# Sorting v of batch 0 straight from its token-major rows, in a Sinkhorn attention and feed-forward kernel

## The chip, the cores and the metric

The kernel runs on one core of one Trainium2 chip. The metric is device time in microseconds (us): 268.45 us is the median of three runs before the change (267.92 to 269.1).

## The reference

A doubly normalised 8x8 matrix P per batch and head mixes the eight 96-token blocks of k and of v. Each block of q then attends to its own mixed block only, and the result goes through a two-layer feed-forward network.

```python
B, H, S, D = 4, 8, 768, 64;  n_blocks = 8;  block = 96
P = sort_net
for _ in range(5):
    P = P - np.max(P, axis=-1, keepdims=True)
    P = np.exp(P)
    P = P / (np.sum(P, axis=-1, keepdims=True) + 1e-09)
    P = P / (np.sum(P, axis=-2, keepdims=True) + 1e-09)
k_sorted = np.einsum('bhij,bhjcd->bhicd', P, k_b)      # k_b, v_b: [B, H, 8, 96, 64]
v_sorted = np.einsum('bhij,bhjcd->bhicd', P, v_b)
scores = (1 / np.sqrt(D)) * np.matmul(q_b, k_sorted.transpose(0, 1, 2, 4, 3))
attn = softmax(scores)                                  # over the 96 keys of the block
x = np.matmul(attn, v_sorted)                           # to [3072 tokens, 512]
h = x @ w_in                                            # [512, 2048]
out = (np.maximum(h, 0) + alpha * np.minimum(h, 0)) @ w_out   # [2048, 512]
```

## The kernel before

**Layout of v.** Each batch of q, k and v is loaded by one DMA (four for batch 3) from GpSimd's queue, which converts float32 to bf16 on the way. It lands as 128 partitions by 3072 elements. A partition is one half of one block of one head: 48 tokens of 64 elements each. For v this tile is `VST` (two of them, used in turn by even and odd batches); within a partition an element of the head dimension, d, recurs every 64 elements.

**Sorting v.** `conv_v(b, u)` copies eight of the 64 values of d from `VST` into `VD`, a tile of 64 rows of d by 64 tokens: the 48 tokens of each d become contiguous, and the 16 elements behind them stay zero from a clearing at the start (the key `VD0`). `prep_v(b, u)` is a group of 16 matmuls: for each of eight d, and for both halves of the blocks, the stationary operand is the 64 elements of this d in `VD`, the moving operand is every second column of `BDK` (P spread as a block-diagonal 128x128 matrix per batch). The two halves go to partitions 0 to 63 and 64 to 127 of a PSUM bank, so the zero tokens fill the rows between. A copy on ScalarE (ACT) or VectorE (DVE), at line 538 (L538, recorded by the profile under the helper's L323), then evicts the bank into `VS`, from which attention takes it. Eight groups, u = 0 to 7, make a batch. For batch 0 they use four banks in turn (psO0, psO1, psP, psY); later batches use psP alone.

**Batch 0 at the start.** Loads of q, k and v of batch 0 come first. Meanwhile the Sinkhorn loop (`sinkhorn`) runs on DVE and ACT, and TensorE (PE) runs fill-in matmuls on an identity matrix (L811), which write psY and are put in PE's holes up to the first group of `prep_v` that uses psY, and again between the first unit of the first feed-forward layer and the first of the second. `prep_q` and `prep_k` (recorded at L486) write the head-dimension-major QTz and KT. Blocks 0 and 1 then go through `attention`: scores (L569), maximum (L575, tile nm), scores once more less the maximum (L590, L581), exponential (L613, tile Es0), product with `VS` (L622), reciprocal and scaling (L627, L630, tile xq), transposition on PE (L645) into xT.

**Feed-forward.** `ffn1` (L666, with L676 on ACT and L679 on DVE) makes one 128-row unit of the hidden layer for a chunk of blocks: two blocks for the first two chunks, four for the others. `ffn2` (L700) makes 128 output tokens. They fill PE beside attention.

**Order.** Nothing is ordered by hand. Every operation is added to a graph with its engine (or `EITHER`: ACT or DVE), an assumed duration, a priority (lower first) and the keys that it reads and writes. `schedule` then walks through time: on the engine that can start first, it takes the operation of lowest priority number among those ready within 60 ns. It models DMAs from GpSimd's queue as one sequence with assumed durations. The result is a fixed order for each engine; every engine runs its order and waits on semaphores, so an operation that waits holds up all behind it on its engine. On GpSimd (POOL) computing operations and DMA issues share one such order.

Priorities around the change: q -98, k -97 and v -96 of batch 0 are loaded; `VD` is cleared at -95.5; `prep_q` -50, `prep_k` -47, the attention scores of blocks 0 and 1 -46.5 and -46.375, `conv_v` -45.5, `prep_v` -45. Then on POOL: clearing QN and loading k of batch 1 at -21, clearing Esb at -20.5, eight loads of q at -20, v of batch 1 at -19, v of batch 2 at -12, k of batch 2 at -11.9. The weights are loaded at -40 to -29. The load of v of batch 2 overwrites the tile of batch 0 and so waits for whatever reads it.

Of the kernel before, what the change touches and what calls it, by code (L numbers as in the profile page):

```python
# [7 lines left out]
AP = bass.AP  # L8
ACTF = mybir.ActivationFunctionType
BF16 = mybir.dt.bfloat16  # L10
# [231 lines left out]
def bass_sinkhorn_attn__then__act_prelu_kernel(  # L242
# [11 lines left out]
    G = _Graph()  # L254
    sems = {e: es.enter_context(nc.semaphore("s_" + e)) for e in ENGS}

    def dma_sem(name):
        return [es.enter_context(nc.semaphore("d_" + name)), 0]

    def sb(name, shape, dt):  # L260
        return es.enter_context(nc.sbuf_tensor(name, shape, dt))
# [4 lines left out]
    PE, ACT, DVE, POOL, SYNC = ("pe",), ("act",), ("dve",), ("pool",), ("sync",)  # L266
# [14 lines left out]
    BDK = sb("BDK", [128, 4, 128], BF16)  # L281
# [8 lines left out]
    QS = [sb("QS0", [128, 3072], BF16)]  # L290
    QN = sb("QN", [128, 6, 8, 128], BF16)
    KS = [sb("KS%d" % n, [128, 3072], BF16) for n in range(2)]
    VST = [sb("VST%d" % n, [128, 3072], BF16) for n in range(2)]
    VD = sb("VD", [128, 64, 64], BF16)
    QTz = [sb("QTz%d" % n, [128, 2, 4, S], BF16) for n in range(2)]
    KT = [sb("KT%d" % n, [128, 4 * NB * BK0], BF16) for n in range(2)]
# [25 lines left out]
    def copy(e, o, i):  # L322
        return e.activation(o, i, ACTF.Copy) if e is nc.scalar else e.tensor_copy(o, i)  # L323

    def t_either(n, mode=1):
# [4 lines left out]
          w=["P"], prio=-100, dma=(dma_sem("sn"), 0))  # L330
# [12 lines left out]
    def paced(g, n):  # L343
        return [(("turned", "turnx")[n % 2], g + n // 2)]
# [22 lines left out]
    def load_kv(t, src, name, sem, g, b, prio):  # L367
        n = 4 if b == 3 else 1
        for x in range(n):
            G.add(POOL, lambda e, x=x: e.dma_start(  # L370
                AP(t[b % 2], x * 3072 // n, [[3072, 128], [1, 3072 // n]]),
                AP(src.tensor, b * HB + x * 3072 // n, [[3072, 128], [1, 3072 // n]])),
                load_us / n, r=paced(g, x) * (b == 3), w=[(name, b % 2), (name, b % 2, x)] if x == 0 else [(name, b % 2, x)],
                prio=prio, dma=(sem[b + x], 0))

    def load_k(b, prio):
        load_kv(KS, k, "KS", d_k, 11, b, prio)

    def load_v(b, prio):
        load_kv(VST, v, "VST", d_v, 9, b, prio)  # L380

    def consts():
        G.add(DVE, lambda e: e.memset(identf[:, :], 1.0), 150, w=["identf"], prio=-90)
        G.add(POOL, lambda e: e.affine_select(identf[:, :], identf[:, :], [[-1, 128]],
                                              AluOpType.is_equal, 0.0, base=0, channel_multiplier=1),
              350, r=["identf"], w=["identf"], prio=-96.5)
        ib = G.add(ACT, lambda e: copy(e, identb[:, :], identf[:, :]), 280, r=["identf"], w=["identb"],
                   prio=-90)
        G.add(DVE, lambda e: e.memset(epst[:, :], EPS), 100, w=["eps"], prio=-89)
        G.add(POOL, lambda e: e.memset(AP(VD, 48, [[4096, 128], [64, 64], [1, 16]]), 0.0), 900,  # L390
              w=["VD0"], prio=-95.5)
        for h in range(H):
            G.add(POOL, lambda e, h=h: e.memset(  # L393
                AP(QN, h * 128 + (1 - h // 4) * 64, [[6144, 128], [1024, 6], [1, 64]]), 0.0),
                400, w=[("QN0", h)], prio=-21)
        G.add(DVE, lambda e: e.memset(AP(VS[1], 64, [[64 * 65, 112], [65, 64]]), 0.125), 200, w=[("VS1", 1)], prio=-30)

        def red(o, src, w):
            G.add(DVE, lambda e: e.reduce_sum(o, src, axis=AxisListType.X), 280, r=["identf"], w=[w],
                  prio=-70)  # L400
        red(AP(mk1, 0, [[16, 128], [2, 8], [1, 2]]),
            AP(identf, 0, [[128, 128], [16, 8], [1, 2], [2, 8]]), "mk1")
        G.add(ACT, lambda e: e.activation(mkh[:, :], mk1[:, :], ACTF.Copy, scale=0.125), 200, r=["mk1"], w=["mkh"],
              prio=-67)
        for n in range(NE):
            G.add(POOL, lambda e, n=n: e.memset(AP(Esb[n], 48, [[1024, 96], [64, 16], [1, 16]]), 0.0), 300,
                  w=[("Epad", n)], prio=-20.5)
        G.add(DVE, lambda e: e.tensor_reduce(mkj[:, :], AP(identf, 0, [[128, 128], [2, 8], [16, 8], [1, 2]]),
                                             AxisListType.XY, AluOpType.add), 280,
              r=["identf"], w=["mkj"], prio=-70)  # L410
        G.add(DVE, lambda e: e.tensor_reduce(one0[:, :], AP(identf, 0, [[128, 112], [64, 2], [1, 48]]),
                                             AxisListType.XY, AluOpType.add), 280,
              r=["identf"], w=["one0"], prio=-70)
        G.add(ACT, lambda e: e.activation(AP(VS[0], 64, [[64 * 65, 112], [65, 64]]), AP(one0, 0, [[1, 112], [0, 64]]),
                                          ACTF.Copy, scale=0.125),
              220, r=["one0"], w=[("VS1", 0)], prio=-60)
        G.add(ACT, lambda e: copy(e, AP(selk, 0, [[512, 32], [16, 32], [1, 16]]),
                                  AP(identf, 0, [[128, 32], [1, 32], [0, 16]])), 600,
              r=["identf"], w=["selk"], prio=-66)
        return ib.idx  # L420
# [93 lines left out]

    def conv_v(b, u, prio):
        o = AP(VD, 8 * u * 64, [[4096, 128], [64, 8], [1, 48]])
        i = AP(VST[b % 2], 8 * u, [[3072, 128], [1, 8], [64, 48]])
        G.add(EITHER, lambda e: copy(e, o, i), {"act": 845, "dve": 480},
              r=[("VST", b % 2)] + [("VST", b % 2, x) for x in range(4)], w=[("VD", u)], prio=prio)

    def prep_v(b, u, prio, bank=BANK_P):
        t, off, row, keys = bank
        n = b % 2

        def f(e):
            inst = None
            for dd in range(8):
                for th in range(2):
                    inst = e.matmul(AP(t, th * 64 * row + off + dd * 64, [[row, 64], [1, 64]]),  # L529
                                    AP(VD, (8 * u + dd) * 64, [[4096, 128], [1, 64]]),  # L530
                                    AP(BDK, b * 128 + th, [[512, 128], [2, 64]]))
            return inst
        op = G.add(PE, f, 8 * 33, r=[("VD", u), "VD0", ("BDK", b)], w=keys, prio=prio)
        if keys == ["psY"]:
            first_y.append(op)
        o = AP(VS[n], 8 * u, [[64 * 65, 112], [65, 64], [1, 8]])
        i = AP(t, off, [[row, 112], [1, 64], [64, 8]])
        G.add(EITHER, lambda e: copy(e, o, i), {"act": 685, "dve": 690}, r=keys + [("VS1", n)], w=[("VS", n, u)],  # L538
              prio=prio)
# [177 lines left out]
    load_k(0, -97)  # L717
    load_v(0, -96)
    ident_op = consts()
    sinkhorn()  # L720
    spread([0], -48)
# [2 lines left out]
    for u in range(6):  # L724
        prep_k(0, u, -47, BANKS0[(u + 1) % 5])
    for u in range(8):
        conv_v(0, u, -45.5)
    for u in range(8):
        prep_v(0, u, -45, (BANK_O + [BANK_P, BANK_Y])[u % 4])
    for p in range(4):  # L730
        G.add(POOL, lambda e, p=p: e.dma_start(  # L731
# [3 lines left out]
    for p in range(2):  # L735
# [6 lines left out]
          r=["alphaR", "identf"], w=PSP, prio=-44)  # L742
    G.add(DVE, lambda e: e.tensor_scalar(out=omaT[:, :], in0=AP(psYP, 512, [[1024, 128], [1, 16]]), scalar1=-1.0,
                                         scalar2=1.0, op0=AluOpType.mult, op1=AluOpType.add), 200,
          r=PSP, w=["omaT"], prio=-44)
# [4 lines left out]
    for ga, gb in chunks:  # L750
        w = gb - ga
# [11 lines left out]
    for g in range(NG + 12):  # L763
# [9 lines left out]
        b, i = g // NB, g % NB  # L773
# [10 lines left out]
        if b + 1 < B:  # L784
            for t in range(6 if b == 0 and i == 1 else 0):
                turn_q(1, t, 2 + t / 2)
            if b > 0 and i < 6:
                turn_q(b + 1, i, 8 * b + 2 + i / 2)
            vu = [(conv_v, b + 1, u) for u in range(3)]
            for u in range(8):  # L790
                vu += [(prep_v, b + 1, u)] + [(conv_v, b + 1, u + 3)] * (u < 5)
            units = [(prep_k, b + 1, u) for u in range(6)]
            units = units + vu if b == 0 else vu + units
            for x in range(len(units)):
                if i == (4 + x * 4 // len(units) if b == 0 else 1 + x * 7 // len(units)):
                    f, *a = units[x]
                    f(*a, x * 5 / len(units) if b == 0 else 8 * b + 2 + x * 5 / len(units))
# [56 lines left out]
```

## Time and profile before

| | us |
|---|---|
| median of three runs | 268.45 (267.92 to 269.1) |
| the profiled execution, its own time | 268.33 |
| its span in the profile | 266.6 |
| PE busy | 243.1 (91%) |
| DVE busy | 173.8 (65%) |
| ACT busy | 158.5 (59%) |
| POOL busy | 38.8 (15%) |
| `conv_v`, all batches: 19 on DVE, 13 on ACT | 0.526 and 0.870 each (medians) |
| v of a batch, from issue to landing (median of three) | 29.2 |
| mean granted clock of PE | 0.966 |

The profile records one execution. Times are counted from the span's start; "busy" excludes waiting, branching and issuing DMAs. PE is matmuls, PEld weight loads, which overlap with them; SP is the engine that issues output stores and transposing DMAs. In a line of the timeline, the first number is the start, the second the length from the first to the last of the "xN" instructions merged in it, and "[... <-X]" gives idle time of the engine just before, with what ended it ("issue": nothing that the profile shows). A letter-digit name such as L529 is a line of the kernel. The clock is the share of full speed that PE was granted.

### The profile page before, as it was taken

The numbers are of one execution on the slowest core, as the hardware profiler recorded it, in microseconds if no ns is written. First come the engines' busy times: TensorE is split into PE (matmuls) and PEld (weight loads), VectorE is DVE, ScalarE is ACT, GpSimd is POOL, SyncE is SP. The second block draws the span as 40 slices with busy tenths as digits, with TensorE's granted clock in tenths as the row PEclk, the third lists the DMA queues.
The fourth block names the chain that finished last, engine by engine and source line by source line (L and its number), as shares of the span: only waits on it lengthen the run. The fifth ranks groups of instructions, "written<-read, shape, count | busy, mean of one in ns | idle before, by whom it ended". The sixth has DMA issues, their size and how long they took to land.

```text
span 266.6 us, 6349 instructions
## 1 busy us (share of the span) xinstructions
PE 243.1 (91%) x2634; PEld 148.4 (56%) x2665; DVE 173.8 (65%) x344; ACT 158.5 (59%) x425; POOL 38.8 (15%) x62
## 2 busy tenths in 40 slices
PE   4797899789999987999999999998998899999995
PEld 1376677556755654555565555554654545555542
DVE  5787667957955976687885757874666666445400
ACT  4385445747887885677795366564757765444411
POOL 8994000000900111064000000000000000000000
PEclk9997599959999999999999999999999999999999
DMA  6999999999976999999897412524524272000122
GB/s 100 216 202 195 201 207 175 212 187 176 88 104 122 123 163 148 242 142 171 105 140 158 59 54 71 123 48 113 122 52 95 46 100 70 23 37 36 39 81 80
DMA packets 76926, 32.17 MB, mean 121 GB/s; under 512 B 67792, under 2 KB 72928, under 8 KB 76896
## 3 DMA queue, kind: packets, MB, share of 16 engines
q0 software_dynamic: 25168, 13.63, 41.8%
q1 hardware_dynamic: 51728, 18.11, 35.6%
q8 instruction: 21, 0.34, 0.5%
q14 instruction: 9, 0.07, 0.1%
HBM read 27.28 MB, written 6.29 MB: 126 GB/s over the span
## 4 chain that ended last, share of the span: by engine, by line
PE 66%; DMA 11%; DVE 8%; POOL 7%; ACT 4%; issue 2%; POOLq 0%
PE psH L666 27%; PE psYP L700 25%; DMA VST<-in_v_dram 11%; PE psS L700 4%; PE psO L622 3%; PE psYP L529 3%; DVE hT L679 3%; POOL QN L352 3%; ACT Esb L602 2%; PE psS L566 2%; PE psYP L486 1%; DVE xq L630 1%; POOL QN L393 1%; POOL w_in_bf L731 1%; ACT t L676 1%
## 5 line engine op out<-in xcount | busy, mean ns | idle before, releaser
L679 DVE SCALAR_TENSOR_TENSOR hT<-t,omaT,psH 128x384 bf16<-128x384 f32 (+1 forms) x139 | 77.1, 571 | 42.7 <-ACT t L676 41.5
L666 PE MATMUL psH<-xT,w_in_bf 128*128 128x384 bf16 (+1 forms) x556 | 98.8, 314 | 2.7 <-DVE hT L679 2.1
L676 ACT ACTIVATE t<-psH 128x384 f32<-128x384 f32 (+1 forms) x139 | 62.2, 465 | 48.6 <-PE psH L666 47.5
L700 PE MATMUL psYP<-w_out_bf,hT 128*128 128x512 bf16 x306 | 79.3, 382 | 5.3 <-DVE hT L679 1.2
L666 PEld LDWEIGHTS psH<-xT,w_in_bf 128*128 128x128 bf16 x556 | 50.2, 99 | 37.1 <-DVE hT L679 7.9
L602 ACT ACTIVATE Esb<-psS,nf 96x96 bf16<-96x96 f32 x192 | 46.2, 342 | 8.3 <-DVE nf L575 8.2
L700 PEld LDWEIGHTS psYP<-w_out_bf,hT 128*128 128x128 bf16 x336 | 31.6, 99 | 33.4 <-DVE outstg L323 2.5
L352 POOL DMA_DIRECT2D QN<-in_q_dram x24 | 20.2, 864 | 45.2 <-DMA QTz<-QN 44.3
L575 DVE TENSOR_REDUCE nf<-psS 96x8 f32<-96x768 f32 x24 | 22.7, 948 | 5.9 <-PE psS L566 5.8
L630 DVE TENSOR_TENSOR xq<-psO,rec 96x512 bf16<-96x512 f32 x31 | 21.3, 686 | 0.9
L323 ACT ACTIVATE outstg<-psYP 128x512 f32<-128x512 f32 x16 | 9.6, 599 | 10.0 <-PE psYP L700 10.0
L529 PE MATMUL psYP<-BDK,VD 128*64 128x64 bf16 x448 | 12.9, 204 | 1.4 <-DVE VS L323 0.9
L811 PE MATMUL psYP<-identb 128*128 128x512 bf16 x36 | 11.1, 445 | 3.4 <-ACT identb L323 3.4
L323 ACT ACTIVATE VS<-psYP 112x512 bf16<-112x512 f32 x15 | 10.3, 685 | 5.7 <-PE psYP L529 5.4
L529 PEld LDWEIGHTS psYP<-BDK,VD 128*64 128x64 bf16 x448 | 9.9, 117 | 6.6 <-issue 1.9
L566 PEld LDWEIGHTS psS<-KT,QTz 128*96 128x96 bf16 x192 | 11.5, 124 | 3.6 <-ACT Esb L602 1.2
L566 PE MATMUL psS<-KT,QTz 128*96 128x96 bf16 x192 | 12.8, 210 | 0.5 <-ACT Esb L602 0.5
L622 PEld LDWEIGHTS psO<-VS,ET 112*96 112x96 bf16 x192 | 11.9, 125 | 2.5
L627 DVE RECIPROCAL rec<-psO 96x8 f32<-96x8 f32 x31 | 6.2, 200 | 10.0 <-PE psO L622 9.7
L622 PE MATMUL psO<-VS,ET 112*96 112x65 bf16 x192 | 12.4, 209 | 0.0
L323 DVE CAST VS<-psYP 112x512 bf16<-112x512 f32 x13 | 9.0, 690 | 4.8 <-PE psYP L529 4.8
L323 ACT ACTIVATE VD<-VST 128x384 bf16<-128x384 bf16 x13 | 10.8, 872 | 0.9 <-PE psYP L529 0.5
(108 smaller groups left out, 179.7 us busy)
## 6 DMA issues: line engine op xcount, KB each, us to landing
out_dram<-outstg SPq DMA_DIRECT2D x24, 256.0 KB, 2.1
KS<-in_k_dram POOLq DMA_DIRECT2D x3, 768.0 KB, 28.6
VST<-in_v_dram POOLq DMA_DIRECT2D x3, 768.0 KB, 29.2
QN<-in_q_dram POOLq DMA_DIRECT2D x24, 96.0 KB, 5.0
w_in_bf<-in_moe_w_in_dram POOLq DMA_DIRECT2D x4, 512.0 KB, 17.4
w_out_bf<-in_moe_w_out_dram POOLq DMA_DIRECT2D x2, 1024.0 KB, 27.3
QS<-in_q_dram POOLq DMA_DIRECT2D x1, 768.0 KB, 6.9
VST<-in_v_dram POOLq DMA_DIRECT2D x4, 192.0 KB, 4.7
```

Of the source, the lines that this page charges most:

```text
L323: return e.activation(o, i, ACTF.Copy) if e is nc.scalar else e.tensor_copy(o, i)
L352: G.add(POOL, lambda e, h=h: e.dma_start(AP(QN, h * 128 + (h // 4) * 64, [[6144, 128], [1024, 6], [1, 64]]), AP(q.tensor, b * HB + h * S * ...
L529: inst = e.matmul(AP(t, th * 64 * row + off + dd * 64, [[row, 64], [1, 64]]), AP(VD, (8 * u + dd) * 64, [[4096, 128], [1, 64]]), AP(BDK, b ...
L566: inst = e.matmul(o, AP(QTz[n], hp * 3072 + h4 * 768 + i * 96, [[6144, 128], [1, 96]]), AP(KT[n], (h4 * 8 + i) * bk, [[ld, 128], [64, 2], ...
L575: G.add(DVE, lambda e: e.tensor_reduce(AP(nx, 0, [[8, 96], [4, 2], [1, 4]]), AP(psX, 0, [[1024, 96], [512, 2], [96, 4], [1, 96]]), AxisLis ...
L602: inst = e.activation(AP(Esb[me], p * 128, [[1024, 96], [64, 2], [1, 48]]), AP(psX, (p // 4) * 512 + (p % 4) * 96, [[1024, 96], [48, 2], [ ...
L622: inst = e.matmul(AP(psZ, hp * 512 + h4 * 68, [[1024, 96], [1, 65]]), AP(ET[me] if far else Es0[m], pos(h4, hp) * 96, [[768, nk], [1, 96]] ...
L630: G.add(DVE, lambda e: e.tensor_tensor(out=AP(xq[me], 0, [[512, 96], [256, 2], [64, 4], [1, 64]]), in0=AP(psZ, 0, [[1024, 96], [512, 2], [ ...
L666: inst = e.matmul(AP(pt, poff, [[1024, 128], [1, n]]), AP(w_in_bf, kt * DFF + ft * 128, [[KT_TILES * DFF, 128], [1, 128]]), AP(xT, kt * XR ...
L676: G.add(ACT, lambda e: e.activation(AP(t1[tb], 0, [[384, 128], [1, n]]), AP(pt, poff, [[1024, 128], [1, n]]), ACTF.Relu, scale=-1.0), t_ac ...
L679: G.add(DVE, lambda e: e.scalar_tensor_tensor(out=AP(hT, ft * RING + tok % RING, [[FT_TILES * RING, 128], [1, n]]), in0=AP(t1[tb], 0, [[38 ...
L700: inst = e.matmul(AP(bank[0], bank[1], [[row, 128], [1, 512]]), AP(hT, ft * RING + tok % RING, [[FT_TILES * RING, 128], [1, 128]]), AP(w_o ...
```

## The change

For batch 0 alone, `prep_v` takes its stationary operand from `VST` itself: the 64 elements that start at d and step by 64. The tile `VST0` is widened from 3072 to 4096 elements a partition, and its last 1024, which are tokens 48 to 63, are cleared at the start by POOL, in the place where `VD` was cleared. The clearing of `VD`, which later batches still need, moves to priority -20.7. The eight `conv_v` of batch 0 are gone. Batches 1 to 3 are sorted as before; batch 2 uses the widened tile through `conv_v`.

```diff
@@ -290,7 +290,7 @@
-    VST = [sb("VST%d" % n, [128, 3072], BF16) for n in range(2)]
+    VST = [sb("VST%d" % n, [128, VP], BF16) for n, VP in ((0, 4096), (1, 3072))]
@@ -368,7 +368,7 @@ def load_kv
-                AP(t[b % 2], x * 3072 // n, [[3072, 128], [1, 3072 // n]]),
+                AP(t[b % 2], x * 3072 // n, [[4096 if name == "VST" and b % 2 == 0 else 3072, 128], [1, 3072 // n]]),
@@ -387,8 +387,10 @@ def consts
+        G.add(POOL, lambda e: e.memset(AP(VST[0], 3072, [[4096, 128], [1, 1024]]), 0.0), 900,
+              w=["VST0"], prio=-95.5)
         G.add(POOL, lambda e: e.memset(AP(VD, 48, [[4096, 128], [64, 64], [1, 16]]), 0.0), 900,
-              w=["VD0"], prio=-95.5)
+              w=["VD0"], prio=-20.7)
@@ -514,7 +516,7 @@ def conv_v
-        i = AP(VST[b % 2], 8 * u, [[3072, 128], [1, 8], [64, 48]])
+        i = AP(VST[b % 2], 8 * u, [[3072 if b % 2 else 4096, 128], [1, 8], [64, 48]])
@@ -527,10 +529,11 @@ def prep_v
                     inst = e.matmul(AP(t, th * 64 * row + off + dd * 64, [[row, 64], [1, 64]]),
+                                    AP(VST[0], 8 * u + dd, [[4096, 128], [64, 64]]) if b == 0 else
                                     AP(VD, (8 * u + dd) * 64, [[4096, 128], [1, 64]]),
                                     AP(BDK, b * 128 + th, [[512, 128], [2, 64]]))
             return inst
-        op = G.add(PE, f, 8 * 33, r=[("VD", u), "VD0", ("BDK", b)], w=keys, prio=prio)
+        op = G.add(PE, f, 8 * 33, r=[("VST", 0), "VST0", ("BDK", 0)] if b == 0 else [("VD", u), "VD0", ("BDK", b)], w=keys, prio=prio)
@@ -723,8 +726,6 @@
-    for u in range(8):
-        conv_v(0, u, -45.5)
     for u in range(8):
         prep_v(0, u, -45, (BANK_O + [BANK_P, BANK_Y])[u % 4])
```

## The prediction

> **What bounds the kernel now.** I read the summary lines of the page first, for which engine is full, and where it is not.
>
> ```profile
> span 266.6 us, 6349 instructions
> PE 243.1 (91%) x2634; PEld 148.4 (56%) x2665; DVE 173.8 (65%) x344; ACT 158.5 (59%) x425; POOL 38.8 (15%) x62
> PE   4797899789999987999999999998998899999995
> PEclk9997599959999999999999999999999999999999
> ```
>
> PE is busy for 91% of the span, so time is made where PE has holes or a slow clock. Each digit is a slice of 6.67 us. The holes stand in slices 0 to 5 (to 40 us) and 9 to 10 (60 to 73 us), and the granted clock is down in slices 3 and 4 and again in slice 8. The change works in slices 2 and 3. The timeline of that stretch comes next, one engine at a time.
>
> ```profile
> 16.84 1.12 DVE L323 COPY VD<-VST 128x384 bf16<-128x384 bf16 x2
> 19.63 1.10 DVE L323 COPY VD<-VST 128x384 bf16<-128x384 bf16 x2
> 20.67 1.27 DVE L323 CAST VS<-psO 112x512 bf16<-112x512 f32 x2
> ...
> 17.32 3.19 ACT L323 ACTIVATE VD<-VST 128x384 bf16<-128x384 bf16 x4
> ...
> 17.96 0.72 PE L529 MATMUL psO<-BDK,VD 128*64 128x64 bf16 x32
> 22.89 0.57 PE L529 MATMUL psO<-BDK,VD 128*64 128x64 bf16 x20 [1.12 <-issue]
> 25.11 0.85 PE L622 MATMUL psO<-VS,Es 112*96 112x65 bf16 x8 [0.16 <-DVE VS L323]
> ```
>
> Columns are start, length, engine, line, operation. Conversions hold DVE and ACT from 16.84 to 20.7, the first eviction of sorted v into VS therefore starts at 20.67, the last ends at 25.05, and the first attention product (L622) starts at 25.11, released by it. PE has a hole of 1.12 us inside this, at 21.77, for which the profile shows no releaser. Third, the chain of waits in order of time, and the table by stretches (columns: stretch, length, busy time and count of PE, PEld, DVE, ACT, POOL, clock, DMA share, GB/s):
>
> ```profile
> 21.36 29.17 DMA VST<-in_v_dram
> 50.53 0.02 issue
> 50.55 2.25 DVE VD L323 x5
> ...
> 20.27:23.67 3.40, 2.10 (x67) 1.84 (x67) 2.43 (x5) 2.80 (x5) 2.73 (x5) 0.95 1.24 206
> 23.67:27.08 3.41, 2.52 (x44) 2.15 (x39) 2.35 (x7) 0.89 (x2) 0.00 (x0) 0.50 1.21 181
> 27.08:30.50 3.42, 2.98 (x27) 2.09 (x27) 2.26 (x5) 1.31 (x3) 0.00 (x0) 0.50 1.22 200
> 30.50:33.90 3.40, 3.40 (x27) 2.49 (x27) 1.75 (x6) 1.36 (x3) 0.00 (x0) 0.55 1.24 207
> 51.06:54.47 3.41, 1.27 (x24) 0.74 (x17) 3.38 (x9) 2.94 (x6) 0.00 (x0) 0.94 1.05 212
> ```
>
> The chain does not go through the start: it runs through the load of v of batch 1, landing at 50.53. So a gain at 25 us has to pass that point. And the clock is at half from about 23.7 to 33.7, after a stretch in which PE was busy 2.10 of 3.40 us.
>
> **The change part by part.** *The conversions* (L726-727) go: four DVE copies, 1.12 + 1.10 = 2.22 us, and four ACT copies, 3.19 us.
>
> *The matmuls* (L529) stay 8 groups of 16; each now waits for the load of v alone. That had landed by 16.84, when the first conversion read it. Three groups can be put where three fill-in matmuls stood (16.71 to 17.47), as their banks (two of psO, psY) are free or nearly so, while the first scores still wait for the KT eviction that ends at 17.42. From here I lay the queues out by hand. A group in a run of two adds 0.72 - 0.44 = 0.28 us, a group by itself about 0.33; I take 0.33 for the old operand.
>
> *The price of the operand.* The stationary operand is now read with a step of 64 elements, 128 bytes; no weight load of this trace does that. Lower end 0: a group whose moving operand steps by two elements (L529) and one with a step of one (L486) both take 0.44 us. It can't be below 0, as the count and size of loads stay. Upper end: ACT takes 0.872 us for the 384 elements of a conversion, read with this step, against 0.49 us for an xT copy of 384 read in order; 0.38/384 = 1.0 ns an element, 64 ns a load, 128 loads: 8.2 us. DVE's two rows (0.526 against 0.36) give 0.43 ns, 28 ns a load, 3.5 us. The nearest row is the same group on PE itself with the whole array at half clock: 0.64 us at 59.04 against 0.44 at full clock. If the step halves the rate of the loads, it costs at most that 0.20 a group, 1.6 us in all; since loads of one half of the array run beside matmuls of the other I take half, 0.10 a group, 0.8 us, and a group of 0.43.
>
> *The queues then.* PE: groups 0, 1 and 3 from 16.84 to 18.13, both scores (0.56) to 18.7, group 2 to 19.1, then 4 and 5 as their banks come free. Evictions cost 0.69 each. ACT takes u0 at 17.5, u3 at 18.3, u2 at 19.3 and u4 to 20.7; DVE takes u1 to 18.6, the two maxima (0.95 each) to 20.4, and u5, u6 and u7 to 22.5. The exponentials (0.82, 0.81) of blocks 0 and 1 follow their maxima and end near 21.5 and 22.4, where they were at 21.2 and 22.06. So VS is full at 22.5, not 25.05, and L622 starts at 22.6: 2.5 us earlier. The hole of 1.12 us has no cause that I can take away, so I keep all of it: **1.4 us**. The point at which this is zero: 2.5 us over eight groups, 0.31 us a group or 19 ns a load above 0.43 with the hole gone, 0.18 us a group with it.
>
> *The clock.* It came back after 30.50:33.90, in which PE had no hole, not after 27.08:30.50, with 2.98 of 3.42. L666 now starts 1.4 us earlier, at 27.8 instead of 29.17, and that earlier stretch is then close to full (30.5 - 27.8 = 2.7, and about 0.5 before it). If the clock returns one stretch sooner, PE, which has no hole there, gains half of 3.4 us, 1.7. I take half of that, **0.85 us**, since 3.2 of 3.42 lies between what did and what did not bring it back.
>
> The Trainium skill gives a rule for this: "TensorE: Matmul & The Clock Gate", Part 1, has the clock decided in free-running windows of 3413 ns. The changes here at 23.7, 33.7 to 33.9 and 54.5 agree, with three and nine such windows between them. By the rule the gain is 1.7 or 0, never 0.85, and the sum below would be 3.1 or 1.4.
>
> A second rule speaks against the change: "SBUF — State Buffer", the box on cachelines under Door 1, wants two hits in each 16-byte line for full bandwidth, and this operand has one. It gives no duration; were the loads to run at half rate with nothing hidden, the price is 1.6 us in place of 0.8 and the sum is 0.8 us smaller.
>
> *POOL.* The clearing of VST0's tail takes the place and size of the old clearing of VD (0.97 us at 3.43). VD's own moves behind the QN clearings; queued behind it on POOL are three Esb clearings, eight q loads, then v of batch 1, k and v of batch 2, all 0.97 us later. I cost that at nothing: v of batch 1 was issued at 21.36 and landed 29.17 us later, with 175 to 212 GB/s in every slice between; it waits for its turn. Should the queue run dry, 0.97 us comes back at 50.5. The load of v of batch 2 waits now for PE's last group instead of a conversion; it is issued about when it was (22.43), and first read at 60.28.
>
> *At 50.5.* The conversions of batch 1 wait there, 0.3 us in ACT. The planner (`schedule`) times loads by a sequence of their own, so with an earlier start it places more work ahead of these conversions rather than pulling them ahead of the load, and there is some: 13 of the 32 feed-forward units of blocks 0 to 3 come after 50 us. I take off **0.25 us** for a longer wait.
>
> Sum: 1.4 + 0.85 - 0.25 = 2.0. The profiled execution took 268.33 us (span 266.6 and 1.7 around it), so 266.3; the median of the runs is 0.12 higher, so **266.4 us**. About 0.5% (1.3 us) is what a measurement of this kernel can tell from no change: faster is below 267.1, slower above 269.8.
>
> **The rivals.** *Absorbed at the load.* PE reaches the conversions of batch 1 early and waits for 50.53. For it: the chain runs through that load, and only the 0.3 us of wait says how tight it is. Against it: PE has work in hand. Time: 268.4, down to 267.3 if the clock alone is kept.
>
> *The step is dear (slower).* Place: the 128 weight loads at 17 to 25 us. Price: by DVE's row 3.5 us, by ACT's 8.2, in place of 0.8. With 3.5 the start is 1.4 - 2.7 = -1.3, and the clock term falls away: 269.8, about 270 as the scores of blocks 0 and 1 are pushed too; with 8.2 it is 1.4 - 7.4 = -6.0: 274.4. It decides from 0.18 us more a group.
>
> *A further stretch at half clock (slower).* The order on PE changes everywhere after 17 us, three fill-ins go, and a stretch like 51.06:54.47 (1.27 of 3.41 busy) can come once more. Price 1.7 us in full work for each, two of them against a gain of 1.4: 270.3.
>
> That the change does nothing isn't a rival: the eight copies are gone by the diff.
>
> **How the numbers follow.** Forecast 0.44, absorbed 0.24, dear step 0.20, clock 0.12. The forecast's own range: 264.5 (2.5 + 1.7 - 0.25 = 3.95, with the hole gone and the clock back early) to 267.3 (1.4 - 0.25 = 1.15, no clock). The whole range goes up over the absorbed case to the two slower ones, 270.5; DVE's price lies inside, ACT's does not. Low end 264.5. Faster: 0.42 of the forecast and 0.04 of the absorbed case, 0.46. Slower: both slower rivals, 0.32. Same: 0.22.
>
> **What would show it.** Right: no copies of VD before 50 us; L529 from about 16.8 at 0.4 to 0.5 us a group; first eviction of VS before 18.5, the last at 22.5 to 23.7; L622 at 22.6 to 23.7; the first ffn unit (L666) before 28; clock back near 30.5; v of batch 1 still landing at 50 to 51. Wrong: groups over 0.6 us, S1 of block 0 after 18.5, VS full after 25, a longer wait of DVE and ACT at 50.5 with PE idle beside it, or new slices of PEclk at 5.

## The result, and the profile after

The changed kernel takes 270.36 us (median of 17 runs, 269.07 to 272.3), against 268.08 us for the kernel before (17 runs, 267.21 to 269.97). The ratio is 1.0094, 95% interval 1.0069 to 1.0119: slower by 0.9%, or 2.3 us. Ratios, here and below, leave out the executions of the slow state (four of the twelve of a_step1 and two of the twelve of a_step1_fill4), and the medians do not; without these executions those two medians are 268.6 and 267.6 us. The profiled execution of the changed kernel took 269.2 us, with a span of 267.5 us and a mean granted clock of 0.974; it is one of the faster of the 17, whose mean clock averages 0.964.

The summary lines of the page after, as they were shown of before:

```profile
span 267.5 us, 6370 instructions
PE 249.0 (93%) x2664; PEld 152.8 (57%) x2664; DVE 172.2 (64%) x342; ACT 155.8 (58%) x419; POOL 39.5 (15%) x63
PE   4899999969999997999899999998998899999995
PEclk9997579999999999999999999999999999999999
```

DVE and ACT lost 1.6 and 2.7 us of work, as the removal of the conversions says. PE gained 5.9 us of busy time, and slice 3, which had 7 tenths, is full now. So the hole in PE was filled, but with what? The timeline after (start, length, engine, line, operation; `prep_v` is now L531, the scores L572 and L593/L584, the attention product L625):

```profile
16.70 2.18 PE L531 MATMUL psO<-BDK,VST 128*64 128x64 bf16 x32
18.70 1.17 PE L531 MATMUL psYP<-BDK,VST 128*64 128x64 bf16 x16
19.79 0.38 PE L572 MATMUL psS<-KT,QTz 64*96 64x96 bf16 x8
...
23.30 2.12 PE L531 MATMUL psYP<-BDK,VST 128*64 128x64 bf16 x32
25.35 0.61 PE L593 MATMUL psS<-QTz,KT 64*112 64x96 bf16 x8
...
28.46 0.85 PE L625 MATMUL psO<-VS,Es 112*96 112x65 bf16 x8
...
17.95 0.69 DVE L323 CAST VS<-psO 112x512 bf16<-112x512 f32 x1 [1.23 <-PE psO L531]
25.45 1.29 DVE L323 CAST VS<-psYP 112x512 bf16<-112x512 f32 x2 [3.14 <-PE psYP L531]
55.74 2.21 DVE L323 COPY VD<-VST 128x384 bf16<-128x384 bf16 x5
```

Three groups do start at 16.70 and the first eviction of VS at 17.95, not 20.67. But two groups take about 2.0 us, where the pair at 17.96 before took 0.55 to the next start: 1.0 us a group. The next work on PE comes 2.00 us after the first pair and 1.09 us after the single group. The first scores start at 19.79 instead of 17.47, the second scores stand behind all eight groups at 25.35 instead of 19.39, DVE waits 3.14 us for the last groups, and the attention product starts at 28.46 instead of 25.11. All eight groups take 8.16 us (16.70 to 19.79 and 20.28 to 25.35), 1.02 each. The reason is in the weight loads. The first line is the answer for the tile VST after, the second that for the tile VD before (columns after the count: least/median/most duration in ns):

```profile
L531 PEld LDWEIGHTS psO<-BDK,VST x64: 202/222/234, 16.7 to 23.1; 128*64 128x64 bf16 x64
```
```profile
L529 PEld LDWEIGHTS psO<-BDK,VD x64: 106/112/114, 18.0 to 23.2; 128*64 128x64 bf16 x64
```

A load itself doubles, from 112 to 222 ns; loads overlap one another, so from start to start it is 2.0 us over 32 = 63 ns, against 0.55 us over 32 = 17 ns in the pair at 17.96 before. The table by stretches after (stretch, length, busy time and count of PE, PEld, DVE, ACT, POOL, clock, DMA share, GB/s):

```profile
20.27:23.67 3.40, 3.40 (x59) 3.39 (x56) 2.04 (x3) 1.54 (x3) 2.33 (x4) 1.00 1.24 203
23.67:27.08 3.41, 3.41 (x52) 3.17 (x52) 1.29 (x2) 0.72 (x2) 1.07 (x2) 0.50 1.12 158
33.90:37.30 3.40, 3.40 (x26) 2.44 (x26) 1.70 (x6) 1.36 (x3) 0.00 (x0) 0.50 1.23 221
57.90:61.30 3.40, 1.76 (x31) 1.07 (x28) 1.48 (x4) 3.25 (x7) 0.00 (x0) 1.00 1.20 143
```

The clock stays at half for four stretches, 23.7 to 37.3, where it was three; the half clock that the kernel before showed from 54.1 to 60.9 (0.50 and 0.56 in two stretches) is missing in this execution. The groups at 23.30 lie almost wholly in a stretch with a clock of 0.50, and their 32 matmuls take 2.05 us to the next instruction, as the first 32 took 2.00 at full clock. Last, the chain of waits does not go through the load of v of batch 1 any more; it goes through the groups themselves:

```profile
16.77 2.11 PE psO L531 x32
20.35 1.10 PE psYP L531 x13
21.45 2.03 PE psO L531 x32
23.48 1.94 PE psYP L531 x32
```

### The profile page after: what moved, and what is told of

The parts are those of the page before. It is cut to its first block, busy times and chain, and to the rows that moved or that the text cites. A ratio compares the mean times of both kernels' runs of the same rounds, so it can differ in the third digit from the quotient of the medians.

```text
span 267.5 us, 6370 instructions
## 1 busy us (share of the span) xinstructions
PE 249.0 (93%) x2664; PEld 152.8 (57%) x2664; DVE 172.2 (64%) x342; ACT 155.8 (58%) x419; POOL 39.5 (15%) x63
## 4 chain that ended last, share of the span: by engine, by line
PE 78%; DVE 13%; ACT 6%; issue 1%; DMA 1%
PE psH L669 27%; PE psYP L703 26%; PE psYP L531 4%; PE psS L703 4%; PE psO L625 4%; DVE hT L682 3%; PE psS L569 3%; ACT Esb L605 2%; DVE xq L633 2%; PE psYP L488 2%; PE psS L584 2%; PE psO L531 2%; ACT t L679 1%; PE psYP L812 1%; PE psS L593 1%
## 5 line engine op out<-in xcount | busy, mean ns | idle before, releaser
L679 ACT ACTIVATE t<-psH 128x384 f32<-128x384 f32 (+1 forms) x139 | 62.5, 466 | 50.5 <-PE psH L669 49.5
L703 PE MATMUL psYP<-w_out_bf,hT 128*128 128x512 bf16 x336 | 84.6, 379 | 2.0 <-DVE outstg L323 1.9
L323 DVE CAST VS<-psYP 112x512 bf16<-112x512 f32 x16 | 11.0, 693 | 7.6 <-PE psYP L531 7.5
L323 ACT ACTIVATE outstg<-psYP 128x512 f32<-128x512 f32 x15 | 9.0, 600 | 8.7 <-PE psYP L703 8.6
L625 PEld LDWEIGHTS psO<-VS,ET 112*96 112x96 bf16 x192 | 11.9, 125 | 2.7
L531 PE MATMUL psYP<-BDK,VD 128*64 128x64 bf16 x384 | 10.6, 198 | 2.3 <-DVE hT L682 1.6
L625 PE MATMUL psO<-VS,ET 112*96 112x65 bf16 x192 | 12.4, 209 | 0.0
L531 PEld LDWEIGHTS psYP<-BDK,VD 128*64 128x64 bf16 x384 | 7.9, 111 | 7.6 <-DVE hT L682 2.3
L323 ACT ACTIVATE VS<-psYP 112x512 bf16<-112x512 f32 x12 | 8.3, 690 | 6.4 <-PE psYP L531 6.3
L703 PE MATMUL psS<-w_out_bf,hT 128*128 128x512 bf16 x48 | 10.5, 379 | 0.0
```

Source lines behind the costliest of these rows:

```text
L625: inst = e.matmul(AP(psZ, hp * 512 + h4 * 68, [[1024, 96], [1, 65]]), AP(ET[me] if far else Es0[m], pos(h4, hp) * 96, [[768, nk], [1, 96]] ...
L679: G.add(ACT, lambda e: e.activation(AP(t1[tb], 0, [[384, 128], [1, n]]), AP(pt, poff, [[1024, 128], [1, n]]), ACTF.Relu, scale=-1.0), t_ac ...
L703: inst = e.matmul(AP(bank[0], bank[1], [[row, 128], [1, 512]]), AP(hT, ft * RING + tok % RING, [[FT_TILES * RING, 128], [1, 128]]), AP(w_o ...
```

## The experiments

All kernels here have one thing in common: the 66 transposing DMAs of batches 1 to 3 (tiles QTz, ET and xT) are plain DMAs, so these batches are computed from untransposed data. The orders on PE, DVE and ACT are those of before, or of after. *b_plain* and *a_plain* are the two kernels with this edit and what it needs beside it (other source patterns, wider tiles Esb and xq, and their clearing on GpSimd):

```diff
-            G.add(SYNC, lambda e: e.dma_start_transpose(
+            G.add(SYNC, lambda e: e.dma_start(
```

> A base for the experiments: the kernel before, with the 66 transposing DMAs of batches 1 to 3 (QTz, ET, xT) made plain DMAs into the same tiles, so batches 1 to 3 are computed from untransposed data (three pads are 1 in place of 0 for that, and GpSimd clears six small tiles after 22 us). The order of every instruction on PE, DVE and ACT is that of the kernel before, and the first of these DMAs is issued at 48 us. Expected by all theories: up to 48 us the profile of the kernel before (L622 at 25.1, groups of L529 at 0.33); the end within 3 us of 268, since plain DMAs land sooner or later than transposing ones.

> The second base: the changed kernel with the same plain DMAs. Expected by all theories: up to 48 us the profile of the changed kernel (groups of 16 at 1.05 us, product of block 0 at 28.5). Against the first base: theory A (dear weight loads) and rival B (order): slower by 1 to 4 us. Rival C (the clock alone): difference follows the share of the run at half clock, 1.7 us for each stretch of 3.4.

Measured: b_plain 268.78 us, 1.0015 (0.9992 to 1.0038) of the kernel before; a_plain 272.09 us, 1.0133 (1.0097 to 1.0169). The first attention product starts at 25.27 and 28.67, as in the originals (25.11, 28.46). The bases carry the loss; it is 1.2% between them. (The profile of a_plain comes from its shortest execution, 270.36 us.)

**Only the step undone (a_step1).** The order is that of after; the stationary operand is read in order, which takes wrong elements of v for batch 0.

```diff
-  AP(VST[0], 8 * u + dd, [[4096, 128], [64, 64]])
+  AP(VST[0], (8 * u + dd) * 64, [[4096, 128], [1, 64]])
```

> The second base with one edit: the stationary operand of batch 0 is read in order (a step of one element in place of 64), so the sorted v of batch 0 is made of the wrong elements; orders, waits, number and size of all instructions are those of the second base. Theory A (the 128-byte step makes a weight load dear, 65 ns in place of 20): a group of 16 takes 0.33 us, the sorted v is complete at 22.5 to 23.7, the product of block 0 starts before 24, and the time is 1 to 3 us below the first base. Rival B (groups ahead of the scores are to blame, whatever they cost): product still after 26 and the time at that of the second base. Rival C (the clock decides, not the start): product early, but the time no lower than the first base's, in step with the share of the run at half clock.

Measured: 269.25 us (265.93 to 271.31), ratio 0.9998 (0.9961 to 1.0034), against 272.09 us for a_plain: the loss is gone. Groups cost 0.29 us again (three from 16.71 to 17.59). But nothing is won over b_plain either, and its timeline on PE shows why:

```profile
18.86 0.42 PE L531 MATMUL psYP<-BDK,VST 128*64 128x64 bf16 x16
22.38 0.64 PE L531 MATMUL psYP<-BDK,VST 128*64 128x64 bf16 x16 [3.10 <-issue]
...
26.05 0.85 PE L625 MATMUL psO<-VS,Es 112*96 112x65 bf16 x8
```

Seven groups are through by 19.28, then PE stands for 3.10 us, released by nothing that the profile shows; in the kernel before the same kind of hole was 1.12 us. The attention product starts at 26.05, later than before. The mean clock of the twelve runs is lower too, 0.965 against 0.972 in b_plain.

**Only the step done (b_step64).** The order and the conversions are those of before; the matmuls of batch 0 read VST0 with the step of 64, wait for it too, and VST0 is widened and its tail cleared as in the change.

```diff
+  AP(VST[0], 8 * u + dd, [[4096, 128], [64, 64]]) if b == 0 else
   AP(VD, (8 * u + dd) * 64, [[4096, 128], [1, 64]]),
```

> The first base with its conversions, waits and orders (one more clearing on GpSimd), and with the one edit that the matmuls of batch 0 read the widened token-major tile with the step of 64; the conversions are made and not used. Theory A: eight groups of 1.05 in place of 0.33, the product of block 0 starts 4 to 5.5 us later than in the first base (29 to 30.5), the time is 2 to 5 us above it. Rival B (the new order costs, not the step): within 0.5% of the first base.

Measured: 272.69 us, ratio 1.0166 (1.0131 to 1.0201). The timeline on PE:

```profile
17.97 2.18 PE L531 MATMUL psO<-BDK,VST 128*64 128x64 bf16 x32
28.84 0.85 PE L625 MATMUL psO<-VS,Es 112*96 112x65 bf16 x8 [0.57 <-DVE VS L323]
```

With the old order the same operand costs the same 1.0 us a group and moves the attention product by 3.6 us (25.27 to 28.84). So the step alone makes the kernel slower, wherever the groups stand.

**The dose (a_steps).** One step for each group, the rest as in after (wrong elements of v for batch 0).

```diff
+  AP(VST[0], dd, [[4096, 128], [(64, 32, 16, 8, 4, 2, 1, 64)[u], 64]])
```

> The second base with another step for each group of batch 0: 64, 32, 16, 8, 4, 2, 1 and 64 elements for u = 0 to 7 (wrong elements of v for batch 0). It looks only at the length of a group of 16. If the price is one for each new 16-byte line: steps of 8 to 64 elements cost the same, about 1.0 us a group, 4 elements (two in a line) about 0.33 to 0.6, 2 and 1 cost 0.33. If it goes with the distance, it falls steadily from 64 to 1. If it belongs to the place in the order, all eight take about 1.0.

Measured, in the timeline on PE. The order is steps 64 and 32, then 16 or 8 alone, the scores, the other of these alone, steps 4 and 2, steps 1 and 64:

```profile
16.71 2.12 PE L531 MATMUL psO<-BDK,VST 128*64 128x64 bf16 x32
18.65 1.14 PE L531 MATMUL psYP<-BDK,VST 128*64 128x64 bf16 x16
...
20.20 1.15 PE L531 MATMUL psYP<-BDK,VST 128*64 128x64 bf16 x16
21.19 0.93 PE L531 MATMUL psO<-BDK,VST 128*64 128x64 bf16 x32
21.95 1.43 PE L531 MATMUL psYP<-BDK,VST 128*64 128x64 bf16 x32
23.31 0.41 PE L593 MATMUL psS<-QTz,KT 64*112 64x96 bf16 x8
```

From start to next start, steps 64 and 32 take 1.94 us together, each of 16 and 8 about 1.0, steps 4 and 2 together 0.76, and steps 1 and 64 together 1.36. The weight loads tell the groups of a pair apart. This is the line of step 4:

```profile
L531 PEld LDWEIGHTS psO<-BDK,VST x16: 157/159/161, 21.1 to 21.6; 128*64 128x64 bf16 x16
```

A load takes 159 ns at step 4, about 113 at steps 2 and 1, and 205 to 228 (medians of the groups) at 8 to 64. Within a group, the matmuls that follow the loads start 29 ns apart at step 4, 16 ns at steps 2 and 1, and 53 to 62 ns at 8 to 64. So the price is nothing at a step of 2, about a third of the full one at 4 (8 bytes), and full from 8 elements (16 bytes) on, where the distance no longer matters. One execution took 268.04 us, beside 268.06 for the kernel before; with one run this says nothing of the time. The Trainium skill, "SBUF — State Buffer", the box on cachelines, wants at least two hits in each 16-byte line for full bandwidth. The full price at step 8, with one hit in a line, agrees; the part paid at step 4, with two, does not, nor does the stride of 8 bf16 that the box calls free. It gives no factor, which is about 59/16 = 3.7 here.

**Where the hole comes from (b_fill4, a_step1_fill4).** The long runs of fill-in matmuls ahead of it are made of four matmuls of 128 columns for each one of 512: 72 more instructions for PE, the same work. In b_plain the hole stands behind 349 or 350 of PE's matmuls, and in a_step1 at 350.

```diff
-        for _ in range(n):
-            inst = e.matmul(psYP[:, 0, :], identb[:, :], AP(identb, 0, [[128, 128], [0, 4], [1, 128]]))
+        for x in range(n if n < 8 else 4 * n):
+            ...
+                inst = e.matmul(AP(psYP, x % 4 * 128, [[1024, 128], [1, 128]]), identb[:, :], identb[:, :])
```

> The first base with one edit: each of the 24 fill-in matmuls before 12 us (two runs of 13 and 11) is made of four of 128 columns in place of one of 512, the same columns in all, so PE's program has 72 more matmuls (144 instructions with their weight loads) ahead of everything after 12 us. Theory H (PE's hole is a wait for the next piece of its own program, at matmul 350 of it, and a piece is asked for when an earlier one is used up): the hole moves 72 matmuls forward, to the first groups of L529 near 18, and is shorter, under 1 us, as the earlier piece is used up sooner; the eight groups then run without a hole, the product of block 0 starts at 24 to 25 in place of 25.1, and the time is 0 to 1.5 us below the first base. Rival T (the hole belongs to the time, 21.8 to 22.9, whatever is run): the hole stays at 21.8 to 22.9 and the time stays. Rival S (it belongs to the instructions of group u = 4): it stays in that group.

> The second base with the stationary operand read in order and the same 72 additional matmuls in the early fill-ins. Without them this kernel had a hole of 3.10 us at matmul 350, from 19.28 to 22.38. Theory H: the hole moves 72 matmuls forward, to about 17.5, and shrinks below 1.5 us; the groups of batch 0 end before 21, the second scores follow at 21, the product of block 0 starts at 23 to 24 in place of 26.05, and the time is 1.5 to 3 us below that kernel at the same clock. Rival T: PE still stands from 19.3 to 22.4.

The timelines on PE, b_fill4 first:

```profile
18.86 0.26 PE L529 MATMUL psYP<-BDK,VD 128*64 128x64 bf16 x5
21.30 0.89 PE L529 MATMUL psYP<-BDK,VD 128*64 128x64 bf16 x27 [2.18 <-issue]
```
```profile
21.33 0.38 PE L572 MATMUL psH<-KT,QTz 64*96 64x96 bf16 x8 [3.04 <-issue]
```

In both the hole moved to a place 72 of the old matmuls earlier: it is bound to a count of instructions, not to an operand or a bank. It does not keep its length: it ends at 21.30 and 21.33, where it ended at 22.87 and 22.38. The earlier PE reaches the same place, the longer it stands. b_fill4 took 271.63 us, 1.0117 (1.0093 to 1.0141); a_step1_fill4 267.79 us, 0.9992 (0.9964 to 1.002).

**The hole without DMA beside it (a_step1_quiet).** In a_step1 all loads after q, k and v of batch 0 wait until the last group of batch 0 is evicted. The end is late because of that; only the start is read.

```diff
-                load_us / 8, r=[("QN0", h)] + paced(13, h // 2) * (b == 3), ...
+                load_us / 8, r=[("QN0", h), ("VS", 0, 7)] + paced(13, h // 2) * (b == 3), ...
```

(The same key is added to what the loads of k and v of batches 1 to 3 and of both weights read.)

> The second base with the stationary operand read in order, and with all loads after q, k and v of batch 0 (both weights, batch 1 and later) held back on GpSimd until the last group of batch 0 is evicted; up to there PE's order is the same. Only the first 24 us are looked at; the end is late by the held loads. Theory Q (PE's hole at matmul 350 is a wait for the next piece of its program, whose transfer stands behind the data transfers): with DMA quiet after 16 us, the hole of 3.10 us at 19.28 is gone or below 0.5 us, the groups end by 19.7, the second scores follow at 19.7. Rival: the piece takes its time whatever else is moved; the hole ends at 21.3 to 22.9 as in all others.

The stretch from 20 to 21 us in the table by stretches (columns as above), a_step1 first and a_step1_quiet second, and then the timeline of a_step1_quiet on PE:

```profile
20.00:21.00 1.00, 0.00 (x0) 0.00 (x0) 0.21 (x1) 0.34 (x1) 1.00 (x2) 1.00 1.24 208
```
```profile
20.00:21.00 1.00, 1.00 (x26) 0.85 (x22) 1.00 (x3) 0.36 (x1) 0.00 (x0) 1.00 0.07 16
```
```profile
19.68 0.44 PE L531 MATMUL psYP<-BDK,VST 128*64 128x64 bf16 x16 [0.39 <-ACT VS L323]
...
21.99 0.53 PE L625 MATMUL psO<-VS,Es 112*96 112x65 bf16 x8
```

With the DMA share at 0.07 instead of 1.24 the hole is gone, and the attention product starts at 21.99: the start that the prediction laid out without a hole was 22.6. (GpSimd, which issues the loads, is idle in that stretch too.) Bound to a count, without an engine as its releaser, and gone with the data loads: I read it as PE waiting for its own instructions, which come by DMA (the page has a queue "instruction" with 21 packets and 0.34 MB). The kept traces hold the times of these packets, 16 KB each. Between 15 and 25 us they have one of them in each kernel with a hole, and the hole ends 1.29 to 1.53 us after that packet has ended:

| kernel | packet ends, us | hole ends, us |
|---|---|---|
| b_fill4 | 19.77 | 21.30 |
| a_step1_fill4 | 19.81 | 21.33 |
| a_told_step1 | 20.85 | 22.17 |
| a_step1 | 21.04 | 22.38 |
| hyb3 | 21.13 | 22.42 |
| b_v1 | 21.33 | 22.74 |
| b_plain | 21.40 | 22.87 |
| before | 21.47 | 22.89 |
| hyb3_v1 | 23.04 | 24.34 |

So the hole goes with this packet. That the packet is late because it stands behind the data loads rests on one pair: it ends at 18.34 in a_step1_quiet, 2.7 us earlier than in a_step1.

**The order (a_told, a_told_step1).** The planner is told 1040 ns for a group of batch 0, not 264, on the order of after; the second kernel has the operand in order.

```diff
-        op = G.add(PE, f, 8 * 33, ...
+        op = G.add(PE, f, 1040 if b == 0 else 8 * 33, ...
```

> The second base with one number changed: the planner is told 1040 ns for a group of batch 0 in place of 264, so it puts the scores of blocks 0 and 1 between the groups instead of behind them. Theory A (dear weight loads): the groups still take 1.05 us each, 8.4 in all, so the sorted v is complete near 26 and the product of block 0 starts at 27 to 28, 0.5 to 1.5 us before the second base; the time is 0 to 1.5 us below it and still above the first base. Rival B (order is the larger part): the product at 25 to 26 and the time at or below the first base.

> The second base with the operand read in order and the planner told 1040 ns for a group of batch 0: cheap groups, with the second scores ahead of the later groups on PE. Only the order differs from the kernel with step 1 alone, in which the second scores stood behind all groups and the hole, and the product of block 0 started at 26.05. If the order is a part of the loss: the exponentials are through before the hole ends, the product starts at 23.5 to 24.5, and the time at equal clock is 1 to 2 us below that kernel, 0.5 to 1.5 below the first base. If not: product at 25.5 to 26.5 and no difference.

Measured: the first and second scores then stand between the groups. With the dear operand the attention product starts at 28.29 (28.67 in a_plain) and the time is 272.45 us, 1.0147 (1.0124 to 1.017): 0.38 us at the start and no gain in the time, as the eight groups fill PE anyway. With the cheap one it starts at 24.76 (26.05 in a_step1): the order was worth 1.3 us at the start. The hole ends at about the same time in both (22.17 and 22.38). The time, 271.63 us, 1.0108 (1.0072 to 1.0143), is nevertheless worse than that of a_step1.

**One group straight (hyb3).** Only u = 3 takes the new operand, in the place of the fill-ins; the seven others are converted as before. VD is cleared early again, and the planner is told 1040 ns for this one group.

```diff
-    ... if b == 0 else
+    ... if b == 0 and u in (3,) else
```

> A try at a version that beats both, with plain DMAs as in the bases: of batch 0 only group u = 3 is sorted straight from the token-major rows (its bank is free early, and it stands where PE ran fill-ins), the other seven are converted as before. It saves one conversion (0.55 us of DVE or 0.8 of ACT) and costs one dear group (1.05 us of PE) near 17, which pushes the first scores by about 0.4 us. Expected: the product of block 0 at 24.7 to 25.3 against 25.1 in the first base, the time within 0.5% of it; the clock decides the rest.

Measured: the product starts at 24.31, 0.96 us earlier than in b_plain (0.44 of it is a shorter hole, 0.66 us), and the first feed-forward unit at 27.91, 1.4 us earlier. The time is 269.52 us, 1.003 (1.0006 to 1.0053). The start gained is lost later. A place to look at is the landing of v of batch 1. Lines of the view of waits from 46 to 62 us (engine and tile that waited, for what, us in total, times, longest), first of b_plain, then of hyb3, then of a_told_step1:

```profile
DVE VD L323 <- DMA VST<-in_v_dram: 0.7, 1, 0.7
```
```profile
DVE VD L323 <- DMA VST<-in_v_dram: 0.8, 1, 0.8
```
```profile
DVE VD L323 <- DMA VST<-in_v_dram: 3.5, 1, 3.5
```

The conversions of batch 1 began at 50.81, 50.76 and 50.60: whatever was won ahead of this load, it lands when it lands. In a_told_step1 DVE stands idle for it. In hyb3 it waits no longer than in b_plain, which fits other work being placed ahead; yet its first scores of batch 1 come at 70.21, where b_plain has 69.97, so the 1.4 us are gone by then.

**An earlier landing (b_v1, hyb3_v1).** The load of v of batch 1 is issued ahead of the eight loads of q, in b_plain and in hyb3.

```diff
-                load_v(1, -19)
+                load_v(1, -20.9)
```

> The first base with one number changed: the load of v of batch 1 is issued ahead of the eight loads of q of batch 1 (priority -20.9 in place of -19), which follow it; a try at a version that beats both. If the landing of v of batch 1 (50.5) is what stops a gain from the start: it lands near 46.5, its conversions follow there, the hole of PE at 51 to 55 gets smaller or moves, and the time is 0 to 2 us below the first base. If PE's later work is the bound anyway: same time within 0.5%. It loses if the later q (transposed at 48, needed by the first scores of batch 1 near 70) arrives too late, which the 20 us between speak against.

> The same change of the order of loads on the kernel that sorts only group u = 3 straight (product of block 0 at 24.31 in place of 25.27, first feed-forward unit 1.4 us earlier, but DVE and ACT then waited 0.8 and 1.1 us at the landing of v of batch 1 and the end was no earlier). If the landing stopped that gain: this kernel is 0.5 to 1.5 us below the one with the load moved alone, and the wait at the landing is below 0.3 us. If the start is lost for other reasons: no difference between the two, or later.

Measured: the conversions on DVE start at 47.56 and 49.70, 3.2 and 1.1 us earlier, and those on ACT at 46.50 and 48.64. The times are 268.91 us, 1.0028 (0.9998 to 1.0058), and 269.12 us, 1.002 (0.9994 to 1.0047): no gain. So the landing alone does not hold the end; what does was not found. In the profiled execution of hyb3_v1, the longest of its twelve (271.41 us), PE's hole grew to 1.97 us, ending at 24.34, and took the earlier start away (26.23).

No version is faster than the kernel before.

## Why the prediction was wrong, point by point

**The price of the operand: the term that failed first.** The sum had 0.33 us a group for the old operand and 0.10 for the step, 0.8 us of price in all. Measured are 1.02 us a group, so the price is 1.02 - 0.33 = 0.69, or 5.5 us for eight. The prediction had two rows with the same access in hand, 28 ns more a load on DVE and 64 ns more on ACT; PE's 63 - 17 = 46 ns lies between them. It put them aside for "the nearest row", the same group at half array clock, and halved that. But a group at half clock is slow in the array, and what the step costs is not: the dear groups cost the same at half clock (2.05 us for two) as at full (2.00). Nor was there an overlap to halve for: the 32 matmuls of a pair take the 2.0 us that their 32 loads take. The upper end of 8.2 us was too high and DVE's 3.5 too low, but either would have made the change slower.

Three of the prediction's own signs of being wrong came: groups over 0.6 us (1.02), the first scores after 18.5 (19.79), and VS full after 25 (25.45 + 1.29 = 26.74).

**The hole: a length kept where an end should have been.** The prediction kept 1.12 us. a_step1 has the cheap operand and still starts the product 0.9 us later than before, since the hole grew to 3.10 us and the second scores stood behind it. Over before, b_plain, a_step1 and the two fill-in kernels the hole's length goes from 1.10 to 3.10 us, its end only from 21.30 to 22.89. So the 2.5 us of the hand layout weren't to be had, even with a free operand; without the hole they were (21.99 in a_step1_quiet). The prediction kept the hole as it saw no cause that it could take away; what stayed was the end. In the changed kernel there is no hole: the place, which is the last group in its order, is reached at about 24.3, after the hole's end in every kernel of that list (the packet ended at 21.08 here). This paid for part of the price.

**The order.** I had the first scores at 18.13 and the second ones among the groups; they stand at 19.79 and 25.35. The planner counted 264 ns for a group that takes 1.0 us, and put the groups first. By a_told this cost 0.4 us at the product on top of dear groups, and by a_told_step1 1.3 us with cheap ones.

Put together at the attention product: a gain of 2.5 without the hole, less 8 x (1.02 - 0.43) = 4.7, is 2.2 us late. Measured is 3.35. I put the remaining 1.15 down to the second scores, which stand behind the groups and run at half clock (L584 0.98 us there, 0.61 at 19.73 before); only the 0.4 of a_told was measured by itself.

**The clock: a gain that became a loss.** I expected the clock back one stretch sooner, for 0.85 us; in the profiled execution it came back one later, at 37.3 instead of 33.6, while the half clock from 54.1 to 60.9 did not occur. The mean clock, averaged over runs, is 0.9642 for the changed kernel (17 runs) and 0.9706 for the kernel before (the 23 runs beside b_plain), and one stretch of 3.41 us at half clock is 0.5 x 3.41/267 = 0.0064 of it: one more on the average. At equal mean clock the change costs 1.35 us (0.974: 269.24 against 267.89) and 1.05 (0.968: 269.83 against 268.78). So of the 2.3 us about 1.2 are work and about 1.1 the clock, as an estimate. Which stretch it is on the average, and that it follows from the later start, isn't shown: with the same dear loads, the profile of a_plain has half clock from 19.8 to 36.9, that of b_step64 from 27.4 to 37.6 only. The third rival named a further half-clock stretch; on the average one did come, but with the dear step, not instead of it.

**At 50.5: a gain is lost on the way, and so is part of a loss.** The deduction of 0.25 us for a longer wait could not be tried by the changed kernel, which comes late. In hyb3 the wait did not grow (1.1 us on ACT and 0.8 on DVE, 1.0 and 0.7 in b_plain), and yet the product came 0.96 us forward and the end not at all. The other way round, the changed kernel is 3.35 us late at the product and 5.2 us at the conversions of batch 1 (55.74), but 1.2 us at the first scores of batch 1 (71.44 against 70.21) and 0.9 at the last scores (213.21 against 212.32). Two things are visible in between: v was there when the conversions came, so nothing waited for it, and the half clock of 54.1 to 60.9 did not occur in the execution that was profiled. What binds the end after 70 us when the start is earlier stays open; b_v1 only rules out the landing as the single bound.

**What held.** The conversions went, and with them 4.3 us of DVE and ACT work; L531 started at 16.70 and the first eviction at 17.95; POOL's later queue shows no cost (the load of v of batch 1 was issued at 21.99, not 21.36, and had landed when the conversions came; that of batch 2 waited 3.11 us for PE, to 25.72, and was read long after). The direction was that of the rival "the step is dear", with its place and its threshold (0.18 us a group, measured 0.59 above 0.43); its times, 270 by DVE's row and 274.4 by ACT's, lie on both sides of 270.36. That 270.36 is so near to the first is partly luck: the price was larger than DVE's row says, 3.35 us at the product, and about 1 us of that did not reach the end.

**Slips.** The prediction places PE's later holes in slices 9 to 10; on the page they are in slices 7 and 8 (47 to 60 us), around the landing at 50.5. Its sums by the rule of the windows, 3.1 and 1.4, leave out the 0.25; they are 2.85 and 1.15. The absorbed case with the clock alone is 268.45 - 0.85 = 267.6, not 267.3. None of these moves the forecast.

## What to carry to other kernels

A layout conversion that is taken away from idle engines isn't free if the engine that is full then reads the awkward layout: look for rows with the same access, on whatever engine, before one with the same instruction, and take them as bounds. Here both bounds said slower. A hole without a visible releaser should be tested for what stays fixed, its length or its end, before a gain is counted through it. And a gain at the start of a kernel need not reach its end: the 0.96 us of hyb3 did not, and an earlier landing of v did not let them through.

## What the runs showed of the hardware that was not expected

- A stationary operand of 64 bf16 elements is loaded 16 ns after the one before at a step of 1 or 2 elements, 29 ns at 4, and 53 to 62 ns at 8 to 64 (a_steps). The granted clock doesn't matter to the dear loads (2.00 us for two groups at 1.00, 2.05 at 0.50).
- PE can stand for 0.45 to 3.1 us at a fixed place in its program (matmul 350 here, 72 earlier when 72 matmuls are put in front) while the DMA engines are full. It goes on 1.29 to 1.53 us after a packet of 16 KB of the queue "instruction", whether that ends at 19.8 or at 23.0 us, and it did not stand where the packet ended at 18.34.
- The clock falls to half behind a stretch in which the profile has PE and its weight loads busy for 3.40 and 3.39 of 3.40 us (20.27 to 23.67), with 59 matmuls in it; in b_step64 it stays at 1.00 behind a stretch with 3.42 and 3.22 of 3.42 (20.28 to 23.70), with 62. So the busy time in the profile doesn't tell what the clock will do. The Trainium skill, "TensorE: Matmul & The Clock Gate", Part 1, has the clock decided in free-running windows of 3413 ns, and four of them fit the stretch at half clock from 23.7 to 37.3; no run here shows what activity they count.
